# Copies of sums moved from GpSimd's queue to SyncE's, in a fused convolution and GELU feed-forward kernel

## The chip, the cores and the metric

The kernel runs on one core of a Trainium2 chip. The metric is the device time of one execution in microseconds (us), the median of several runs. A core has five engines that work side by side and meet only through semaphores: TensorE (PE: matrix products; its weight loads are listed as PEld), VectorE (DVE), ScalarE (ACT), GpSimd (POOL) and SyncE (SP). Transfers (DMAs) are issued by SP, ACT or POOL, in the order of that engine's program, and are carried out by 16 DMA engines that all queues share. A transfer tells of its landing by a semaphore.

## The reference

The input x has 8 sequences of 4096 tokens of 192 values. A causal convolution over 7 tokens comes first, whose weights are a softmax over the 7 taps, one set for each of 8 heads of 24 values. Then a feed-forward layer: 192 to 2048, exact GELU, 2048 to 192.

```
w = exp(w - max(w)); w = w / sum(w)                 # over the 7 taps of a head
x = sum over k of w[head, k] * x[token - 6 + k]     # zeros ahead of a sequence
h = x @ w_in                                        # 32768 x 192 @ 192 x 2048
g = 0.5 * h * (1 + erf(h / sqrt(2)))
out = g @ w_out                                     # 32768 x 2048 @ 2048 x 192
```

## The kernel before

The tokens are split into two halves of 16384, and both halves go through the core together: six blocks of 256 tokens of each half, then 29 blocks of 512, blocks 0 to 34. A block of 512 has 16 slots. In a slot TensorE makes 128 hidden columns for 512 tokens of both halves (`mm1`, line 991, into one of two buffers `hp`), and ScalarE applies GELU to them (line 896, into `gT`). Between the slots TensorE works on the second product of the block before, into four banks `ob`. So one block's second product runs beside the next block's first.

For each block VectorE transposes x (line 747), makes the taps of the convolution (line 775; ScalarE makes a first one, line 864), and brings the results of the second product to `osb` (lines 376 and 560), from where SyncE stores them.

Every second block from 8 to 32 (the list `ST`, 13 blocks) does its second product in a transformed way that needs fewer matrix products: instead of all products of parts of `gT` with parts of the weights, it multiplies sums of parts with sums of weights (`mm2_s`, line 1129). The rest take the plain way (`mm2_t`, line 1069). In what follows m is a transformed block; its sums are made while its own slots run, and TensorE uses them beside the slots of block m+1. A pair is block m and block m+1.

The sums are called S1, S3 (four parts each), Dn and S4 (two parts each) and lie in the buffers `sst`. S1 and S3 add two pieces of `gT`; Dn adds a piece of `gT` to S1; S4 adds one to Dn. Most parts are made by VectorE (`st_add`, line 487). Five of the parts of S1 and S3 are made by transfers instead (`BY_DMA`): a copy of one piece into `sst` (`st_dma` with h = 0, line 494) and then a transfer that adds the other piece onto it (h = 1, line 497). The copy waits for the GELU that makes its piece, the add for the copy's landing. TensorE waits for the add's landing before it uses that part (`wait_add`).

What each engine does in what order is fixed:

- GpSimd's list is sorted by a pair (block, slot). For each m it holds the five copies and five adds by `DMAS`: first number the place within block m, then sum, part, and copy (0) or add (1). Between them stand `halo` (lines 663 and 669), which carries six columns of x over to the next block, and `st_move`: a move of half a tile `p5s` at (m+1, 8.5) (line 504), and two later moves, `gsm` and `tq`, at (m+2, 2) and (m+2, 3).
- VectorE's order is written out by hand in `ORDER`, one letter an operation: c a convolution tap, t a transpose, 1, 3, d and 4 a part of S1, S3, Dn and S4, p a step of `st_post`, e a result brought out. `st_post` step 1 (line 538) waits for the landing of `p5s`; step 2 (line 541) must be done before TensorE begins the plain second product of block m+1.
- SyncE's list is also sorted by (block, place). In the steady part it holds for each pair: load of block m+4, store of m-2, load of m+5, store of m-1, each of four transfers of 192 KB. Before each of the four it waits until TensorE has finished the first slot of block m+1:

```
for at, op, n in sorted(work, key=lambda q: q[0]):
    if at[0] - 1 in ST:
        sp.wait_ge(S_MM1, SL0[at[0]] + 1)
    op(sp, n)
```

A load waits for its buffer (three of them, `xin`), a store for its results; VectorE waits for a store's landing before it writes the same `osb` (two of them) again.

Of the kernel before, what the change touches and what calls it, by code (L numbers as in the profile page):

```python
# [11 lines left out]
def bass_lightweight_conv__then__act_gelu_exact_kernel(  # L12
# [53 lines left out]
    SL0 = [sum(NSL[:n]) for n in range(NB + 1)]  # L66
# [5 lines left out]
    ST = list(range(M0 + 2, M1, 2))  # L72
# [43 lines left out]
    def sem(name):  # L116
        return es.enter_context(nc.semaphore(name))

    def ap(t, off, pat):
        return bass.AP(t, off, pat)  # L120

    with es:
# [53 lines left out]
        S_MM1 = sem("S_MM1")  # L176
# [10 lines left out]
        S_AC = sem("S_AC")  # L187
        S_DP = sem("S_DP")
        BY_DMA = [("S3", 0), ("S1", 0), ("S3", 1), ("S1", 1), ("S3", 2)]
        DMAS = [(3, "S3", 0, 0), (4, "S1", 0, 0), (7, "S3", 1, 0), (8, "S1", 1, 0), (8.1, "S1", 0, 1), (8.2, "S3", 0, 1),  # L190
                (9, "S1", 1, 1), (11, "S3", 2, 0), (11.1, "S3", 1, 1), (12, "S3", 2, 1)]
        S_CP = {k: sem("S_CP_%s_%d" % k) for k in BY_DMA}
        S_AD = {k: sem("S_AD_%s_%d" % k) for k in BY_DMA}
        S_PS = sem("S_PS")
# [66 lines left out]
        def part(q):  # L261

            return FQ * (0, 4, 2)[q], [[NP * F, 64], *([[F, NP]] if q < 2 else [[4 * FQ, 2 * NP]]), [1, FQ]]


        def cast(e, n, p):
            e.wait_ge(S_TR, NP * n + p + 1)
            dst = ap(xTb[PC[n]], p * XB + HX, [[NP * XB, 128], [1, WS[n]]])
            src = ap(xT[n % 2], p * XW + HX, [[NP * XW, 128], [1, WS[n]]])
            if n == 0:  # L270
                ins = e.activation(out=dst, in_=src, func=AF.Copy)
            else:
                ins = e.tensor_copy(dst, src)
            ins.then_inc(S_CAST[PC[n]])

        def dup(e, q, hf):

            c0, pat = part(q)
            e.wait_ge(S_WIN[(hf, 2 + 3 * hf, 3 + hf)[q]], 16)
            e.tensor_copy(  # L280
                ap(win, 64 * (1 - hf) * NP * F + c0 + FQ, pat), ap(win, 64 * hf * NP * F + c0, pat)
            ).then_inc(S_DUPP if (q, hf) == (0, 1) else S_DUPE)

        def trd(n):

            return NP * (n + 1) if n < 2 else 2 * NP + n - 1

        def cvd(n):

            return sum(NCV - 2 * (m in K0) for m in range(n + 1) if m not in PC)  # L290
# [100 lines left out]
        for (hf, cg), names in TILES.items():  # L391
            at = 0.0
# [6 lines left out]
        for e, (at, hf, cg, u, k) in enumerate(EVENTS):  # L399
            name = "DE" if u[0] in "DE" else u if u != "P3" else u + "LU"[cg]  # L400
# [161 lines left out]
        def load(e, n, qs=(0, 2, 1, 3), sm=None):  # L562
            mb = WS[n] // 32
            if n >= NX:
                e.wait_ge(S_TR, trd(n - NX))
            for q in qs:
                off = ((q // 2) * HALF + OFF[n]) * D + DQ * (q % 2)
                dst = [[TB // 32 * DQ, 32], [DQ, mb], [1, DQ]]
                src = [[D, 32], [32 * D, mb], [1, DQ]]
                e.dma_start(  # L570
                    ap(xin[n % NX], 32 * q * (TB // 32 * DQ), dst), ap(xt, off, src)
                ).then_inc(sm or S_XIN[n % NX], 16)

        def store(e, m):
# [28 lines left out]
        TAPS = ((5, 8, 11), (10, 12, 15))  # L603
        ORDER = (
            "tccccccccccccctccctccccccccccccwtcwcccccccccccwwwwctcccccccccccctcccccccccccccccccccccccccettceccccc"
            "cccccccccetccccecccccccetcecc1ccde1ed344ccccccpctpcpeccccccccpccececet1ccd3e1ed44ccccccpcccptpcecccc"
            "ccccpccececet1ccd3e1ed44ccccccpcccptpceccccccccpccececet1ccd3e1ed44ccccccpcccptpceccccccccpccececet1"
            "ccd3e1ed44ccccccpcccptpceccccccccpccececet1ccd3e1ed44ccccccpcccptpceccccccccpccececet1ccd3e1ed44cccc"
            "ccpcccptpceccccccccpccececet1ccd3e1ed44ccccccpcccptpceccccccccpccececet1ccd3e1ed44ccccccpcccptpceccc"
# [5 lines left out]
        @block.gpsimd  # L615
        def _(g):
            def win_in(q, hf, sm):
                c0, pat = part(q)
                g.dma_start(
                    ap(win, 64 * hf * NP * F + c0, pat), ap(wint, c0 + FQ * hf, pat)  # L620
                ).then_inc(sm, 16)

            g.wait_ge(S_MSET, 1)
            for hf in range(2):
                m = idb[64 * hf : 64 * hf + 64, :]
                g.affine_select(
                    out=m,
                    in_=m,
                    compare_op=ALU.is_equal,
                    fill=0.0,  # L630
                    base=0,
                    pattern=[[-1, 64]],
                    channel_multiplier=1,
                ).then_inc(S_IDN)
            g.wait_ge(S_IDN, 2)
            g.memset(wnm[:, :], 0.0).then_inc(S_WNM)
            g.memset(ap(xTb[0], HF, [[NP * XB, 128], [XB, NP], [1, HB]]), 0.0).then_inc(S_HALO)
            for q in range(2):
                for hf in range(2):
                    win_in(q, hf, S_WIN[(hf, 2 + 3 * hf)[q]])  # L640
            g.wait_ge(S_PRO, 9)
            g.tensor_tensor(
                ap(dg, 3 * 64, [[KS * 64, 128], [64, KS - 3], [1, 64]]),
                ap(idb, 0, [[64, 128], [0, KS - 3], [1, 64]]),
                ap(wcol, 3, [[32, 128], [1, KS - 3], [0, 64]]),
                ALU.mult,
            ).then_inc(S_DG)

            def wout_in(k):
                g0, gs = ((0, 1), (4, 1), (2, 4), (3, 4))[k]  # L650
                g.dma_start(
                    ap(wout, 2 * g0 * C, [[NF * C, 128], [2 * gs * C, 2], [1, 2 * C]]),
                    ap(woutt, 256 * g0 * C, [[2 * C, 128], [256 * gs * C, 2], [1, 2 * C]]),
                ).then_inc(S_WOUT[k], 16)

            def halo(n):

                t, tw = (xTb[PC[n]], XB) if n in PC else (xT[n % 2], XW)
                dst = ap(t, HF, [[NP * tw, 128], [tw, NP], [1, HB]])
                if n >= 4:  # L660
                    g.wait_ge(S_CV, cvd(n - 2))
                if OFF[n] % SEQ == 0:
                    g.memset(dst, 0.0).then_inc(S_HALO)
                    return
                g.wait_ge(S_TR, trd(n - 1))
                src = ap(
                    xT[(n - 1) % 2], HF + WS[n - 1], [[NP * XW, 128], [XW, NP], [1, HB]]
                )
                g.tensor_copy(dst, src).then_inc(S_HALO)  # L669

            win_in(2, 0, S_WIN[3])
            load(g, 2, (0,), S_XP)
            halo(1)
            g.wait_ge(S_HALO, 2)
            dup(g, 0, 1)
            win_in(2, 1, S_WIN[4])
            wout_in(0)
            load(g, 2, (2,), S_XP)
            g.wait_ge(S_DUPP, 1)
            cast(g, 1, 0)  # L680
            cast(g, 1, 1)
            load(g, 2, (1,), S_XP)
            wout_in(1)
            cast(g, 1, 2)
            load(g, 2, (3,), S_XP)
            wout_in(2)
            wout_in(3)
            halo(2)
            work = [((n - 2, 0), halo, n) for n in range(3, NB)]
            for m in ST:  # L690
                for at, name, q, h in DMAS:
                    work.append(((m, at), st_dma, g, m, name, q, h))
                work += [((m + 1, 8.5), st_move, g, m, 0), ((m + 2, 2), st_move, g, m, 1), ((m + 2, 3), st_move, g, m, 2)]
            for _, op, *rest in sorted(work, key=lambda q: q[0]):
                op(*rest)
# [498 lines left out]
        @block.sync  # L1194
        def _(sp):
            sp.dma_start(wsb[:, :], ap(wt, 0, [[KS, H], [1, KS]])).then_inc(S_WSB, 16)
            load(sp, 0, (0, 1))

            sp.wait_ge(S_PRO, 2)
            load(sp, 1)  # L1200
            sp.wait_ge(S_WOUT[3], 16)
            load(sp, 3)
            work = [((n - 3, 0), load, n) for n in range(4, ST[0] + 4)]
            work += [((p + 1, 1), store, p) for p in range(ST[0] - 2)]
            for m in [*ST, ST[-1] + 2]:
                work += [((m + 1, k), load, m + 4 + k) for k in range(2) if m + 4 + k < NB]
                work += [((m + 1, k + 0.5), store, m - 2 + k) for k in range(2) if m - 2 + k < M1]
            work += [((NB + 1, 0), store, p) for p in range(ST[-1] + 2, M1)]
            for at, op, n in sorted(work, key=lambda q: q[0]):
                if at[0] - 1 in ST:  # L1210
                    sp.wait_ge(S_MM1, SL0[at[0]] + 1)
                op(sp, n)
            for g in range(NG[NB - 1]):
                store_half(sp, g, 0)
            for s in range(2):
                sp.wait_ge(S_OUT[s], OUTS[NB - 1 if (NB - 1) % 2 == s else NB - 2])
# [28 lines left out]
```

## Time and profile before

| | |
|---|---|
| runs | 675.85, 672.76 and 675.66 us; median 675.66 |
| profiled execution | 671.07 us, of which the span of its instructions 669.3 |
| busy in the span | PE 663.9, DVE 612.1, ACT 594.3, POOL 189.6 us |
| copies, line 494 | 65, of 256 KB; issue 0.80 us each (mean) |
| adds, line 497 | 65, of 256 KB; issue 1.42 us each (mean) |
| copies and adds, issue to landing | 2.4 / 3.9 / 6.4 us (least, median, most) |
| loads of x and stores on SyncE, issue to landing | medians 4.8 and 4.6 us for 192 KB |

The profile is of one execution. Each engine's busy time, the idle time ahead of an instruction and what ended it are given; the chain is the run of work that ended last, followed back from the end. TensorE's clock was granted in full throughout (1.000). For a transfer the profile has the time in which the engine issued it and the moment at which it landed. A group of rows with `x3` is three instructions told together.

### The profile page before, as it was taken

To read this page: it belongs to the slowest core of one execution; us is meant where nothing else is said; L and a number is where in the kernel's file an instruction comes from. 1 tells how busy PE (TensorE), PEld (TensorE's weight loads), DVE (VectorE), ACT (ScalarE), POOL (GpSimd) and SP (SyncE) were. 2 spreads that over 40 slices of the span, in tenths; PEclk is the share of its full clock that TensorE was granted. 3 is DMA by queue.
4 is the path that set the end of the run, shared out by engine and by line. 5 is a ranking of instruction groups with operands and counts; after the bars stand their busy time and mean duration, and the time that the engine had idled before them with its cause. 6 is when DMAs were issued, how large, how long until landed. Compare 5 with 4: busy or idle time off the path is not lost.

```text
span 669.3 us, 27462 instructions
## 1 busy us (share of the span) xinstructions
PE 663.9 (99%) x12504; PEld 487.6 (73%) x12504; DVE 612.1 (91%) x704; ACT 594.3 (89%) x681; POOL 189.6 (28%) x230
## 2 busy tenths in 40 slices
PE   9999999999999999999999999999999999999998
PEld 8999655565655767678787777877767776777667
DVE  6999998889999999999999999999999999999621
ACT  8999988898998989989898998989979899898882
POOL 7000702315042250511505124150421504224000
PEclk9999999999999999999999999999999999999999
DMA  9435361967939479494886939569394693936333
GB/s 154 122 89 129 72 108 56 183 132 165 201 103 204 109 159 181 120 197 117 159 163 155 205 91 187 128 160 211 96 198 104 154 205 104 196 87 141 87 73 95
DMA packets 159075, 93.72 MB, mean 140 GB/s; under 512 B 129088, under 2 KB 152448, under 8 KB 158960
## 3 DMA queue, kind: packets, MB, share of 16 engines
q1 hardware_dynamic: 129136, 49.37, 35.5%
q0 software_dynamic: 28704, 42.02, 29.7%
q8 instruction: 98, 1.61, 1.0%
q10 hardware_dynamic: 1120, 0.59, 0.3%
q14 instruction: 17, 0.14, 0.1%
HBM read 28.31 MB, written 25.17 MB: 80 GB/s over the span
## 4 chain that ended last, share of the span: by engine, by line
PE 91%; DMA 4%; POOL 2%; issue 1%; ACT 1%; POOLq 0%
PE hp L991 46%; PE ob L1069 21%; PE ob L1129 17%; PE ob L1031 5%; DMA sst<-gT 4%; POOL sst L497 2%; PE ob L1185 1%; PE hp L1185 1%; PE hp L913 1%; POOL sst L494 1%; ACT gT L896 0%; PE ob L933 0%; PE ob L991 0%; ACT xc L243 0%; ACT osb L350 0%
## 5 line engine op out<-in xcount | busy, mean ns | idle before, releaser
L896 ACT ACTIVATE gT<-hp 128x1024 bf16<-128x1024 f32 x510 | 514.1, 1021 | 61.0 <-PE hp L991 54.7
L991 PE MATMUL hp<-xc,win 64*64 64x512 bf16 (+2 forms) x6036 | 440.1, 366 | 0.1
L775 DVE SCALAR_TENSOR_TENSOR acc<-xT,wcol,acc 128x1024 f32<-128x1024 f32 (+1 forms) x330 | 298.7, 972 | 4.6 <-ACT acc L864 3.9
L991 PEld LDWEIGHTS hp<-xc,win 64*64 64x64 bf16 (+1 forms) x6036 | 231.6, 106 | 90.9 <-ACT gT L896 7.8
L1069 PE MATMUL ob<-gT,wout 64*64 64x512 bf16 x2880 | 205.7, 376 | 0.0
L1129 PE MATMUL ob<-gT,wout 64*64 64x512 bf16 x1248 | 167.3, 376 | 0.0
L1069 PEld LDWEIGHTS ob<-gT,wout 64*64 64x64 bf16 x2880 | 113.2, 118 | 46.4
L1129 PE MATMUL ob<-sst,wst 64*64 64x512 bf16 x624 | 129.6, 376 | 2.1 <-DMA sst<-gT 2.1
L1129 PEld LDWEIGHTS ob<-gT,wout 64*64 64x64 bf16 x1248 | 83.6, 118 | 24.9
L497 POOL DMA_DIRECT2D sst<-gT x65 | 84.3, 1417 | 36.8 <-DMA sst<-gT 31.9
L747 DVE STREAM_TRANSPOSE xT<-xin 128x1536 f32<-128x1536 f32 (+2 forms) x39 | 74.7, 1925 | 1.6 <-DMA xin<-in_x_dram 1.4
L494 POOL DMA_DIRECT2D sst<-gT x65 | 52.2, 803 | 73.0 <-ACT gT L896 72.7
L775 DVE SCALAR_TENSOR_TENSOR xc<-xT,wcol,acc 128x1024 bf16<-128x1024 f32 (+1 forms) x66 | 61.6, 958 | 0.1
L487 DVE TENSOR_TENSOR sst<-gT,sst 128x2048 bf16<-128x2048 bf16 x52 | 61.4, 1231 | 0.1
L864 ACT ACTIVATE acc<-xT,wcol 128x512 f32<-128x512 f32 (+1 forms) x87 | 61.1, 702 | 0.0
L1129 PEld LDWEIGHTS ob<-sst,wst 64*64 64x64 bf16 x624 | 53.2, 107 | 7.7 <-DMA sst<-gT 3.5
L669 POOL COPY xT<-xT 128x18 f32<-128x18 f32 x30 | 28.0, 932 | 106.0 <-DVE xc L775 101.2
L1129 PE MATMUL ob<-gT,wst 64*64 64x512 bf16 x208 | 57.5, 376 | 0.0
L376 DVE STREAM_TRANSPOSE osb<-ob 128x512 f32<-128x512 f32 x45 | 40.6, 905 | 12.3 <-PE ob L1069 12.3
L1129 PE MATMUL ob<-sst,wout 64*64 64x256 bf16 x416 | 45.2, 269 | 0.0
L504 POOL DMA_DIRECT2D p5s<-p5s x13 | 7.4, 570 | 132.7 <-ACT p5s L525 132.7
L1031 PE MATMUL ob<-wout,gT 64*128 64x192 bf16 x768 | 41.9, 243 | 0.0
(74 smaller groups left out, 323.1 us busy)
## 6 DMA issues: line engine op xcount, KB each, us to landing
sst<-gT POOLq DMA_DIRECT2D x130, 256.0 KB, 3.9
out_dram<-osb SPq DMA_DIRECT2D x124, 192.0 KB, 4.6
xin<-in_x_dram SPq DMA_DIRECT2D x116, 192.0 KB, 4.8
tq<-uu POOLq DMA_DIRECT2D x13, 256.0 KB, 4.0
xin<-in_x_dram SPq DMA_DIRECT2D x18, 96.0 KB, 2.4
gsm<-uu POOLq DMA_DIRECT2D x13, 128.0 KB, 2.2
p5s<-p5s POOLq DMA_DIRECT2D x13, 64.0 KB, 4.8
wout<-in_moe_w_out_dram POOLq DMA_DIRECT2D x4, 192.0 KB, 4.5
```

The costliest lines, as they stand in the source:

```text
L376: v.transpose(osb_t(m, j), bank(BK[m][j])).then_inc(S_EV)
L487: v.tensor_tensor(out, one, two, ALU.add).then_inc(S_SA[NS.index(name)])
L494: e.dma_start(out, one).then_inc(S_CP[name, q], 16)
L497: e.dma_start(out, two, accum_op=ALU.add).then_inc(S_AD[name, q], 16)
L747: v.transpose(out, src).then_inc(S_TR)
L775: ins = v.scalar_tensor_tensor(dst, src, wk, a, op0=ALU.mult, op1=ALU.add)
L864: a.activation(out=acc[n % 2][:, p * TB : p * TB + w], in_=ap(xT[n % 2], p * XW + HX, [[NP * XW, 128], [1, w]]), func=AF.Copy, scale=wcol[ ...
L896: a.activation(out=ap(gT[n % 2], i * c * 2 * w, dst), in_=ap(ob, 2 * TB, [[4 * TB, 128], *src[1:]]) if u < SL0[1] and u % 3 == 2 else ap(h ...
L991: ins = t.matmul(hbuf(u, slice(fo, fo + fw), o, w), ap(win, f1, [[NP * F, 64], [2, fw]]), xc[n % 2][r, p * TB : p * TB + w], start=(p == 0 ...
L1031: ins = t.matmul(bb[sub], gT[m % 2][r, c0 : c0 + 128], wout[r, CH[sub][i] * C : (CH[sub][i] + 1) * C], start=(ph == 0 and k == 0), stop=(p ...
L1069: ins = t.matmul(bank(BK[m][j], slice(64 * h, 64 * h + 64), w), ap(wout, 64 * hf * NF * C + CH[h][i] * C + j, [[NF * C, 64], [NP, 64]],), ...
L1129: ins = t.matmul(bank(BK[m][bk], slice(64 * cg, 64 * cg + 64), w), wt_, a[r, c0 : c0 + w], start=(e == mine[0]), stop=(e in (mine[-1], GRO ...
```

## The change

The copies leave GpSimd's list and go to SyncE's, at the same places within block m. GpSimd keeps the adds only, in the order S3 part 0, S1 part 0, S1 part 1, S3 part 1, S3 part 2. SyncE's loads and stores of a pair wait for the fourth slot of block m+1 instead of the first; its copies do not wait for a slot, only for their GELU. In VectorE's order two letters change places, in the first transformed block alone: the first part of Dn comes ahead of one tap.

```diff
-        DMAS = [(3, "S3", 0, 0), (4, "S1", 0, 0), (7, "S3", 1, 0), (8, "S1", 1, 0), (8.1, "S1", 0, 1), (8.2, "S3", 0, 1),
-                (9, "S1", 1, 1), (11, "S3", 2, 0), (11.1, "S3", 1, 1), (12, "S3", 2, 1)]
+        COPIES = [(3, "S3", 0), (4, "S1", 0), (7, "S3", 1), (8, "S1", 1), (11, "S3", 2)]
+        ADDS = [(5, "S3", 0), (6, "S1", 0), (9, "S1", 1), (10, "S3", 1), (12.5, "S3", 2)]
...
-            "cccccccccetccccecccccccetcecc1ccde1ed344ccccccpctpcpeccccccccpccececet1ccd3e1ed44ccccccpcccptpcecccc"
+            "cccccccccetccccecccccccetcecc1cdce1ed344ccccccpctpcpeccccccccpccececet1ccd3e1ed44ccccccpcccptpcecccc"
...
-                for at, name, q, h in DMAS:
-                    work.append(((m, at), st_dma, g, m, name, q, h))
+                work += [((m, at), st_dma, g, m, name, q, 1) for at, name, q in ADDS]
...
+            work += [((m, at), st_dma, m, name, q, 0) for m in ST for at, name, q in COPIES]
...
-            for at, op, n in sorted(work, key=lambda q: q[0]):
+            for at, op, *rest in sorted(work, key=lambda q: q[0]):
                 if at[0] - 1 in ST:
-                    sp.wait_ge(S_MM1, SL0[at[0]] + 1)
-                op(sp, n)
+                    sp.wait_ge(S_MM1, SL0[at[0]] + 4)
+                op(sp, *rest)
```

## The prediction

> **What bounds the kernel now.** I read the page first, then the chain in order of time, the waits, and the timelines of POOL, SyncE, VectorE and TensorE over one pair of blocks. The page:
>
> ```profile
> PE 663.9 (99%) x12504; PEld 487.6 (73%) x12504; DVE 612.1 (91%) x704; ACT 594.3 (89%) x681; POOL 189.6 (28%) x230
> PE 91%; DMA 4%; POOL 2%; issue 1%; ACT 1%; POOLq 0%
> ```
>
> TensorE is hardly ever idle, so at most a few us can be won. The 4% of DMA and 2% of POOL in the chain look like 40 us, but most of that ran beside a busy TensorE: the chain only went through it where a wait ended last. The true loss is read from the rhythm of the chain:
>
> ```profile
> 110.18 0.86 PE ob L1069 x16
> ...
> 232.84 0.86 PE ob L1069 x16
> ...
> 273.43 0.86 PE ob L1069 x16
> ...
> 641.36 0.86 PE ob L1069 x16
> ```
>
> A pair of blocks takes 273.43 - 232.84 = 40.59 us undisturbed. Between 110.18 and 641.36 lie 13 pairs in 531.18 us; 13 x 40.59 is 527.67. So 3.5 us are lost to waits. The waits name them (us in total, times, longest):
>
> ```profile
> PEld ob L1129 <- DMA sst<-gT: 3.5, 3, 1.7
> DVE tq L538 <- DMA p5s<-p5s: 5.5, 8, 1.2
> ```
>
> Three waits of the weight loader on a transferred sum, 3.5 us, are all of it. The second line is on no path yet and returns below. How a sum comes to be late, in an undisturbed pair that begins at 431.14 (its transformed block m, then block m+1 from 451.67):
>
> ```profile
> 440.25 0.71 POOL L494 DMA_DIRECT2D sst<-gT  x1 [3.38 <-ACT gT L896]
> 441.55 0.71 POOL L494 DMA_DIRECT2D sst<-gT  x1 [0.59 <-ACT gT L896]
> 442.25 3.70 POOL L497 DMA_DIRECT2D sst<-gT  x3
> 445.66 1.04 POOL L494 DMA_DIRECT2D sst<-gT  x1
> 446.39 1.52 POOL L497 DMA_DIRECT2D sst<-gT  x1
> 450.47 1.18 POOL L497 DMA_DIRECT2D sst<-gT  x1 [2.56 <-DMA sst<-gT]
> ```
>
> L494 is a copy, L497 an add. The last copy (third part of S3) goes out at 445.66, behind three adds of the same queue; POOL then idles 2.56 us until it has landed, 450.2, and the last add goes out at 450.47. It lands 4.5 us later, 455.0 by the trace's landing times. TensorE asks for it at about 456.5: in the pair begun at 471.72 the loader waited 1.7 us until 498.80, so it had asked at 497.1, 25.4 us into the pair. So the margin is 1.5 us. In that pair the add started 1.7 us later than here (492.75) and took 6.00 us to land, and the margin was gone.
>
> **The change, part by part.**
>
> Copies on SyncE. A copy waits only for the gelu that makes its data; these end in this pair at 434.8, 436.0, 440.0, 441.3 and about 445.4. SyncE is free then: its last store of a pair goes out 34.7 us into the pair, so at 424.5 for the pair before (three slots later, 428.2), and has landed by 428.0 (431.7). POOL loses five issues of 0.72 us, 3.6 us a pair; POOL is 28% busy, so this alone is worth nothing. What counts is that the last copy is no longer in line behind adds. Its landing is shown nowhere for SyncE's ring. Bounds: 2.1 us (fastest load on that ring, half the size) and 6.6 us (slowest); the same copy on POOL's ring takes 2.4 at its fastest and 4.5 here. I take 3.3, nearest to the copy's own undisturbed row, with something for the two adds in flight. It lands at 445.4 + 3.3 = 448.7 instead of 450.2. At 6.6 it would land at 452.0.
>
> Adds as soon as their copy has landed. They are in the order S3, S1, S1, S3, S3; each costs POOL 1.25 us. With copies landed at 438, 439, 443, 444.3 and 448.7 POOL is never behind: the third and fourth are issued 444.3 to 446.8, the last at 448.8. It lands at 453.3 instead of 455.0: 1.7 us more margin, 3.2 in all. With the bound of 6.6 the add lands at 456.6, and the margin is gone. The waiting add holds up on POOL only the copying of six columns to the next block (L669, L663), which came after the last add before too. SyncE's waits hold up only copies and the next loads.
>
> A page of the Trainium skill speaks against this part: by "DMA: Bandwidth & Descriptors", section "Issuing engines are not separate DMA queues", transfers of all issuers run on the same 16 engines and a second issuer saves only issue time. By it the last sum comes 0.3 us earlier (445.66 against 445.4), and about 3 us of the lost 3.5 stay. I go by the 2.56 us of POOL's wait and by 4.5 against 2.4 us for the same copy, which say that the queue's order costs more than the issue.
>
> x and results three slots later. SyncE's 16 transfers of a pair (4 loads, 4 stores, twice) begin at 451.66, with the first slot of block m+1; the fourth slot ends 3.7 us later, 455.3. They fill the DMA engines:
>
> ```profile
> 431.14:451.67 20.53, 20.53 (x386) 15.54 (x382) 20.53 (x23) 18.39 (x21) 11.22 (x13) 1.00 0.59 137
> 451.67:471.72 20.05, 20.05 (x393) 15.40 (x388) 18.83 (x21) 18.80 (x22) 0.88 (x3) 1.00 0.94 176
> ```
>
> (columns: PE, PEld, DVE, ACT, POOL busy, clock, DMA share, GB/s.) The DMA share is 0.94 in block m+1 and 0.59 in block m. Later transfers leave the last add alone, worth nothing beyond the 3.5 us. What covers the delay: loads land 8.4 to 9.6 us before VectorE transposes them (5.8 in the first pair, 7.0 in the last), so at least 2.1 us are left; stores land 8.1 to 10.3 us before their buffer is written again, so 4.4 are left. Were that cover gone, each us late would be a us of VectorE's, which has about 1 us of idle time a pair.
>
> The one other thing in that traffic is the half-width move p5s (L504):
>
> ```profile
> 467.37 0.42 DVE L538 TENSOR_TENSOR tq<-ob,p5s 64x256 f32<-64x256 f32 x1 [1.09 <-DMA p5s<-p5s]
> ...
> 470.07 0.43 DVE L541 TENSOR_TENSOR tq<-ob,p5s 64x256 f32<-64x256 f32 x1
> ```
>
> ```profile
> 471.29 0.86 PE L1069 MATMUL ob<-gT,wout 64*64 64x512 bf16 x12
> ```
>
> ```profile
> DMA to landing us min/median/max: 1.9/4.8/5.2
> ```
>
> The first two rows are VectorE's timeline, the third TensorE's, the last the landing times of the tile p5s. VectorE sits idle until p5s lands (36.2 us into the pair); after it come a transpose and L541, which ends at 470.50 and must be done before TensorE's L1069 matmuls at 471.29. That is 0.8 us of slack. The move's issue stays at 31.1 us into the pair, where SyncE's own transfers now take 4.4 us to land; shifted by 3.7 us it meets the state of 27.4 us, where they take 5.0 to 5.1. So p5s lands 0.6 us later, still inside 0.8; without the last add in the engines it may be less. Bounds: 0.3 us earlier and 1.9 later (the slowest store, 6.1, plus the 0.5 by which p5s lags SyncE's). For pairs that scatter above 0.8 I put 0.5 us in all.
>
> A rule would strike this term out: by "DMA: Bandwidth & Descriptors", section "Queues, rings and completion order", each DMA engine takes turns between queues packet by packet, so a small move need not stand behind a long ring. The trace disagrees: 1.9 us where the ring was empty, 4.8 in traffic. By the rule the sum would be 0.5 us lower.
>
> The swapped step in VectorE's order (first transformed block only) puts one sum of 1.2 us ahead of one tap of 0.9 us. VectorE has idled 1.7 and 1.4 us in that block: nothing, or 0.3 us either way.
>
> Sum: 671.07 (span 669.3 and 1.8 around it) - 3.5 + 0.5 = 668.1 us for the profiled execution.
>
> **Against the median.** The runs shown are 672.76 to 675.85, median 675.66, 4.6 above the profiled one. No view says where these 4.6 us lie. If around the program, the new median is 675.66 - 3.0 = 672.7; if they are more of the same waits (0.35 us a pair), it is 668.1. Spread of 3 us between runs of one program speaks for waits in part; I take the middle, 670.5.
>
> **The rivals.** A change of 0.5% (3.4 us) is about what a measurement of this kernel can tell from none.
>
> First, the gain is real but too small: the waits go only partly, or the 4.6 us are fixed. For it: three waits in 13 pairs are all there is to see. 673 to 677.
>
> Second, slower: p5s. If it lands d later, each of 12 pairs stalls TensorE by d - 0.8 (the last pair's traffic is shorter, 8 transfers). At d = 1.9 that is 13 us, 683 us; it decides from d = 1.2, where 12 x 0.4 eats the gain. For it: 0.8 us is thin and VectorE has no other idle time, so the delay also reaches its own sums. Against: the growth from 4.4 to 5.1.
>
> Third, SyncE's ring is slow for copies (6.6 us), so that the last sum lands 1.6 us later than before. With 1.6 added to the 13 landings of this trace (22.9 to 27.0 us into their pairs, against 25.4) the waits come to 10 us instead of 3.5: 682 us. Against: the ring is empty when copies go out.
>
> **How the numbers follow.** Forecast 0.58 (667 to 673, of which 0.04 within 0.5%), first rival 0.24, second 0.12, third 0.06. Under 672.3 is faster: 0.54; up to 679 the same: 0.28 and 0.01 of each slower case, 0.30; the rest slower, 0.16. For 8 in 10: 666 (all waits gone, p5s as by its early bound) to 677 (first rival whole, little of the others).
>
> **What would show it.** Right: no TensorE wait on a transferred sum; the last add about 17.7 us into a pair instead of 19.3; SyncE's loads from 24.2; p5s still landing by 36.8 and L541 ending before L1069 asks; pairs of 40.6 us throughout. Wrong: a pair longer than 40.6 with TensorE released by VectorE's L541 (second rival) or by a sum's DMA (third), or equal pairs and an unchanged median (first).

## The result

The changed kernel takes 683.13 us (median of 4 runs, 681.37 to 684.25) against 675.41 us before in the same comparison: the ratio is 1.012, with a 95% interval of 1.0084 to 1.0156. The forecast was 670.5 us, range 666 to 677, with 16% for slower. It was wrong, in size and in sign. The profiled execution of the changed kernel has a span of 679.6 us, 10.3 more than the one of before.

In the changed kernel's line numbers, line 991 of before is 990, 1069 is 1068 and 1129 is 1128. Two lines of its page, and four rows of its chain in order of time:

```profile
PE 669.1 (98%) x12504; PEld 500.7 (74%) x12504; DVE 613.5 (90%) x704; ACT 594.5 (87%) x681; POOL 143.3 (21%) x165
PE 65%; DMA 7%; DVE 5%; ACT 1%; issue 1%; DVEq 0%
```

```profile
194.27 0.86 PE ob L1068 x16
...
235.66 0.86 PE ob L1068 x16
276.25 0.86 PE ob L1068 x16
...
610.54 0.86 PE ob L1068 x16
```

The ten pairs between 194.27 and 610.54 take 41.63 us each, 1.04 more than the undisturbed 40.59. One of them, from 235.66 to 276.25, takes 40.59: the floor has not moved. Taken over all 13 pairs by the starts of the blocks' first GELUs, 13.3 us are lost where 3.4 were lost before; the rest of the 10.3 is 0.4 us ahead of the first transformed block. VectorE has entered the chain (5%), and the waits say where (us in total, times, longest):

```profile
POOL sst L497 <- DMA sst<-gT: 140.1, 28, 15.3
DVE sst L487 <- DMA sst<-gT: 15.1, 12, 1.8
PEld ob L1128 <- DVE tq L534: 9.3, 12, 1.3
PEld ob L1128 <- DVE sst L487: 8.1, 11, 1.3
...
DVE tq L538 <- DMA p5s<-p5s: 2.4, 4, 1.0
...
PEld ob L1128 <- DMA sst<-gT: 0.2, 1, 0.2
```

The wait that the change was to remove is gone: TensorE's loader waits 0.2 us for transferred sums instead of 3.5. In its place VectorE waits 15.1 us for a transferred sum, which was no wait worth listing before, and TensorE then waits for VectorE at two places: for a part of a sum made by VectorE (line 487; the fourth part of S1) and for the step of line 534 ten us later. VectorE's own slack, its wait for `p5s`, has shrunk from 5.5 us to 2.4.

What VectorE waits for is the add of S1 part 1: the first part of Dn needs both transferred parts of S1. The timelines of GpSimd, SyncE and VectorE in the pair that begins at 397.90:

```profile
405.80 2.44 POOL L497 DMA_DIRECT2D sst<-gT  x2 [4.45 <-DMA sst<-gT]
414.34 3.65 POOL L497 DMA_DIRECT2D sst<-gT  x3 [6.10 <-DMA sst<-gT]
```

```profile
401.56 11.18 SPq L494 DMA_DIRECT2D sst<-gT  x5
```

```profile
415.01 0.76 DVE L487 TENSOR_TENSOR sst<-gT 128x1024 bf16<-128x1024 bf16 x1
415.57 2.05 DVE L774 SCALAR_TENSOR_TENSOR acc<-xT,wcol,acc 128x512 f32<-128x512 f32 x2
418.14 1.23 DVE L487 TENSOR_TENSOR sst<-gT,sst 128x2048 bf16<-128x2048 bf16 x1 [0.51 <-DMA sst<-gT]
```

SyncE issues the five copies at their GELUs, without a wait of its own. The two adds of 405.80 (7.9 us into the pair; before, adds began at 11.1) start early, as intended. But the copy of S1 part 1, issued at 408.04, lands only at 414.06, and GpSimd stands idle for 6.10 us before the next three adds go out together. The add of S1 part 1 lands at 418.02, and VectorE has waited for it. The DMA engines are left partly idle just then: their share is 0.58 in the changed kernel and 0.98 in the one before. The same stretch of a pair, 16 to 20 us from its start, in the changed kernel and in the one before (PE, PEld, DVE, ACT, POOL busy, clock, DMA share, GB/s):

```profile
413.90:417.90 4.00, 4.00 (x80) 3.07 (x76) 3.73 (x4) 3.40 (x4) 3.56 (x4) 1.00 0.58 105
```

```profile
406.40:410.40 4.00, 4.00 (x80) 3.04 (x76) 4.00 (x5) 3.40 (x4) 1.66 (x3) 1.00 0.98 193
```

Medians over the 13 pairs, in us from the start of the pair, by the landing times in the traces:

| | before | changed | forecast |
|---|---|---|---|
| adds begin | 11.1 | 7.9 | 6.9 |
| copy of S1 part 1: issue, landing | 10.4, 13.4 | 10.1, 15.8 | 10.1, 13.2 |
| add of S1 part 1 lands | 17.8 | 19.9 | not worked out |
| first part of Dn begins on VectorE | 19.2 | 20.1 | not worked out |
| copy of S3 part 2 lands | 19.0 | 16.8 | 17.6 |
| add of S3 part 2: issue, landing | 19.3, 23.9 | 17.6, 23.1 | 17.7, 22.2 |

The undisturbed pair (from 230.71) is the one in which the add of S1 part 1 landed earliest, at 18.8; its copy had landed at 14.8.

Theory A, formed from this: the two early adds lie in the DMA engines ahead of the later copies; the copy of S1 part 1 lands late, so does its add, VectorE waits for it and TensorE pays. Against it stand theory B, that copies are slow on SyncE's ring in themselves, and theory C, that the later loads and stores do the harm.

### The profile page after: what moved, and what is told of

It is laid out like the page before. It is cut to its first block, busy times and chain, and to the rows that moved or that the text cites. A ratio compares the mean times of both kernels' runs of the same rounds, so it can differ in the third digit from the quotient of the medians.

```text
span 679.6 us, 27462 instructions
## 1 busy us (share of the span) xinstructions
PE 669.1 (98%) x12504; PEld 500.7 (74%) x12504; DVE 613.5 (90%) x704; ACT 594.5 (87%) x681; POOL 143.3 (21%) x165
## 4 chain that ended last, share of the span: by engine, by line
PE 65%; DMA 7%; DVE 5%; ACT 1%; issue 1%; DVEq 0%
PE hp L990 32%; PE ob L1128 16%; PE ob L1068 16%; DMA sst<-gT 7%; DVE sst L487 2%; DVE tq L534 1%; ACT gT L895 1%; PE ob L1184 1%; PE hp L1184 1%; DVE osb L376 1%; DVE acc L774 0%; DVE xc L774 0%; ACT osb L350 0%; DVEq L458 0%
## 5 line engine op out<-in xcount | busy, mean ns | idle before, releaser
L990 PE MATMUL hp<-xc,win 64*64 64x512 bf16 (+2 forms) x6036 | 463.6, 366 | 0.4 <-DVE xc L774 0.3
L990 PEld LDWEIGHTS hp<-xc,win 64*64 64x64 bf16 (+1 forms) x6036 | 246.6, 106 | 84.8 <-ACT gT L895 7.6
L1068 PE MATMUL ob<-gT,wout 64*64 64x512 bf16 x2880 | 209.1, 376 | 0.0
L1128 PE MATMUL ob<-gT,wout 64*64 64x512 bf16 x1248 | 183.6, 378 | 0.0
L1068 PEld LDWEIGHTS ob<-gT,wout 64*64 64x64 bf16 x2880 | 122.5, 118 | 37.5
L1128 PE MATMUL ob<-sst,wst 64*64 64x512 bf16 x624 | 131.8, 377 | 3.1 <-DVE sst L487 3.1
L497 POOL DMA_DIRECT2D sst<-gT x65 | 79.2, 1520 | 140.2 <-DMA sst<-gT 140.1
L1128 PEld LDWEIGHTS ob<-gT,wout 64*64 64x64 bf16 x1248 | 89.8, 118 | 16.1
L487 DVE TENSOR_TENSOR sst<-gT,sst 128x2048 bf16<-128x2048 bf16 x52 | 60.8, 1208 | 15.1 <-DMA sst<-gT 15.1
L1128 PEld LDWEIGHTS ob<-sst,wst 64*64 64x64 bf16 x624 | 52.2, 107 | 15.3 <-DVE sst L487 8.1
L669 POOL COPY xT<-xT 128x18 f32<-128x18 f32 x30 | 33.3, 1109 | 114.3 <-DVE xc L774 109.0
L1128 PE MATMUL ob<-sst,wout 64*64 64x256 bf16 x416 | 46.6, 269 | 0.0
L1128 PEld LDWEIGHTS ob<-sst,wout 64*64 64x64 bf16 x416 | 37.7, 119 | 1.0
```

What stands on the lines that cost most here:

```text
L487: v.tensor_tensor(out, one, two, ALU.add).then_inc(S_SA[NS.index(name)])
L497: e.dma_start(out, two, accum_op=ALU.add).then_inc(S_AD[name, q], 16)
L990: ins = t.matmul(hbuf(u, slice(fo, fo + fw), o, w), ap(win, f1, [[NP * F, 64], [2, fw]]), xc[n % 2][r, p * TB : p * TB + w], start=(p == 0 ...
L1068: ins = t.matmul(bank(BK[m][j], slice(64 * h, 64 * h + 64), w), ap(wout, 64 * hf * NF * C + CH[h][i] * C + j, [[NF * C, 64], [NP, 64]],), ...
L1128: ins = t.matmul(bank(BK[m][bk], slice(64 * cg, 64 * cg + 64), w), wt_, a[r, c0 : c0 + w], start=(e == mine[0]), stop=(e in (mine[-1], GRO ...
```

## The experiments

Ratios are to the kernel before on the same chip, with 95% intervals. "Lost" is the sum over the 13 pairs above the undisturbed lengths of their second blocks (20.05 us each), in the profiled execution: 3.4 us before, 13.3 in the changed kernel.

**Adds held back.**

```diff
-        ADDS = [(5, "S3", 0), (6, "S1", 0), (9, "S1", 1), (10, "S3", 1), (12.5, "S3", 2)]
+        ADDS = [(5, "S1", 1), (6, "S1", 0), (9, "S3", 0), (10, "S3", 1), (12.5, "S3", 2)]
```

> The changed kernel, with its adds in the order S1 part 1, S1 part 0, S3 part 0, S3 part 1, S3 part 2, so that no add goes out before the copy of S1 part 1 has landed. Theory A (the adds that now start at 8 to 9 us into a pair fill the DMA engines, the copy of S1 part 1 lands at 16 instead of 13.3 us, its add at 20 instead of 17.8, VectorE waits for it 1.3 us a pair and TensorE then waits for VectorE twice): that copy lands by 13.5, its add by 17.5, VectorE waits for no add, span 666 to 671 us instead of 679.6. Theory B (a copy on SyncE's ring is slow in itself): the copy still lands at about 16, all five adds are later still, span 685 us or more. Theory C (the later loads and stores do the harm): span 677 to 682, as in the changed kernel.

690.77 us, ratio 1.0249 (1.0197 to 1.0300); lost 21.6 us. A miss: the time is what theory B forecast, and the copy and its add land a little later than theory A said. And yet the copy answers: with no add ahead it lands at 13.8, 3.6 us after its issue instead of 5.7, and not at 16 as by theory B. Theory B is refuted on this point. What I had overlooked is the rest of the queue:

```profile
417.71 6.12 POOL L497 DMA_DIRECT2D sst<-gT  x5 [10.41 <-DMA sst<-gT]
```

All five adds now go out in one run, and land at 18.3, 20.8, 22.2, 23.6 and 24.9 us: after the first two, one every 1.3 to 1.5 us. The first part of Dn also needs the add of S1 part 0, now the second, and begins at 20.9; TensorE waits 7.5 us for transferred sums as well.

**Loads and stores from the first slot again.**

```diff
-                    sp.wait_ge(S_MM1, SL0[at[0]] + 4)
+                    sp.wait_ge(S_MM1, SL0[at[0]] + 1)
```

> The changed kernel, with loads and stores issued from the first slot of block m+1 again, as before the change. Theory A: the add of S1 part 1 still lands at about 20 us into a pair, VectorE still waits 1 to 1.5 us for it; time 681 to 690 us, since the last adds now meet the loads. Theory C: back to the time before, 672 to 677 us. Theory B says the same as A here.

682.80 us, ratio 1.0124 (1.0075 to 1.0174); VectorE waits 15.3 us for sums, the add of S1 part 1 lands at 20.2. As A said; theory C is refuted.

**The later loads and stores alone**, on the kernel before:

```diff
-                    sp.wait_ge(S_MM1, SL0[at[0]] + 1)
+                    sp.wait_ge(S_MM1, SL0[at[0]] + 4)
```

> The kernel before, with one change alone: loads and stores three slots later. Theory A: the sums land as before or earlier (the last add meets no loads), TensorE's waits for transferred sums (3.5 us) go, VectorE's p5s waits stay about 1 us; span 665.5 to 668 us instead of 669.3. Theory C: slower than before, span 674 to 680, with TensorE or VectorE waiting for p5s or x. Theory B: as A.

670.28 us, ratio 0.9938 (0.9916 to 0.9960); lost 1.6 us. TensorE's loader waits 0.2 us for transferred sums. The span of the profiled execution, 669.6, missed the range for a reason of its own: its first transformed block began at 107.0 us instead of 105.1. This part of the change makes the kernel faster.

**VectorE's order altered**, so that it comes to the first part of Dn later. In eleven of the thirteen transformed blocks as shown here, and in the first of them the swap is undone:

```diff
-1ccd3e1ed44
+1cc3de1ed44
```

> The changed kernel, with VectorE's order altered: the last part of S3, which needs no transfer, comes before the first part of Dn, which needs the add of S1 part 1 (and the swap in the first transformed block is undone). Transfers are as in the changed kernel. Theory A: the add still lands at about 20 us, but VectorE comes to it only at about 20.2 and waits at most 0.3 us; TensorE's waits for VectorE (8 us for the fourth part of S1 and 9 us for the step of line 534) go mostly; span 667 to 672. If the wait on that add were not what delays TensorE, the span stays at 677 to 682.

677.37 us, ratio 1.0030 (0.9997 to 1.0062); lost 9.7 us. Half a hit. VectorE waits 5.9 us for sums instead of 15.1, and 3.2 us more for the GELU that the last part of S3 needs; TensorE's wait on its sums falls from 8.1 to 4.2 us, but that on line 534 stays at 8.2. VectorE is still 0.9 us later than before when it has done its sums (27.3 against 26.5 us into the pair), and line 534 has no slack for that. The span of the profiled execution, 678.0, lies outside the range for theory A and inside the one for its rival; as VectorE's wait went only in part, this run alone does not decide between them.

**One add ahead instead of two.**

```diff
-        ADDS = [(5, "S3", 0), (6, "S1", 0), (9, "S1", 1), (10, "S3", 1), (12.5, "S3", 2)]
+        ADDS = [(5, "S1", 0), (6, "S1", 1), (9, "S3", 0), (10, "S3", 1), (12.5, "S3", 2)]
```

> The changed kernel, with its adds in the order S1 part 0, S1 part 1, S3 part 0, S3 part 1, S3 part 2: one add instead of two lies in the DMA engines ahead of the copy of S1 part 1. Theory A, as the held adds left it (copy of S1 part 1 at 13.8 with no add ahead, 15.8 with two, 13.4 before; the first part of Dn needs both adds of S1): that copy lands at 14.3 to 15.0, its add at 18.3 to 19.0, the add of S1 part 0 long before, VectorE waits 0 to 0.3 us a pair instead of 1.2, time 670 to 675 us, better than the changed kernel's 683. Against A, if the add of S1 part 1 is late because every add on this queue now takes longer whatever lies ahead: it lands at 20 again and the time stays at 680 to 685.

678.62 us, ratio 1.0063 (1.0034 to 1.0092); lost 9.4 us. The direction of the copy is A's, the rest was missed: the copy lands at 15.1, just beyond the range given, but its add at 19.8, hardly earlier than in the changed kernel, and VectorE still waits 10.5 us for sums. The reason given against A is not it: this add takes 4.3 us from issue to landing, against 4.2 in the changed kernel and 4.1 before (medians). It is late because it is issued late, at 15.5. From issue to landing this copy takes 3.6 us with no add ahead, 5.0 with one and 5.7 with two: the first does two thirds of the harm.

**VectorE held, transfers untouched**, on the kernel before:

```diff
-            v.wait_ge(S_GELU, done)
+            v.wait_ge(S_GELU, SL0[m] + NF if (name, q) == ("Dn", 0) else done)
```

> The kernel before, all transfers as they were, with VectorE's first part of Dn held in every transformed block until that block's last GELU, 20.5 us into the pair, where it had begun at 19.2 and in the changed kernel at 20.1. No transfer is touched. Second half of theory A (a wait of VectorE at this place, whatever its cause, is paid by TensorE at the fourth part of S1 and at the step of line 534): VectorE waits 1.2 to 1.4 us a pair, the 13 pairs lose 12 to 17 us instead of 3.4, time 683 to 690 us. If TensorE lost its time to something else in the change: 673 to 678 us.

687.02 us, ratio 1.0190 (1.0149 to 1.0231); lost 18.9 us. Its waits:

```profile
DVE sst L487 <- ACT gT L896: 22.1, 13, 1.9
...
PEld ob L1129 <- DVE sst L487: 10.9, 13, 0.9
PEld ob L1129 <- DVE tq L534: 8.6, 10, 1.3
```

No transfer was touched, and the same two waits of TensorE appear as in the changed kernel, with VectorE's idle time of 22.1 us ahead of them (1.7 a pair, more than the 1.2 to 1.4 expected, hence the larger loss). The second half of A is shown: idle time of VectorE at this place is paid by TensorE for the most part; 15 us more are lost for 22 us of it.

**Adds at their old times, copies on SyncE, loads late.**

```diff
-        ADDS = [(5, "S3", 0), (6, "S1", 0), (9, "S1", 1), (10, "S3", 1), (12.5, "S3", 2)]
+        ADDS = [(8.1, "S1", 0), (8.2, "S3", 0), (9, "S1", 1), (11.1, "S3", 1), (12, "S3", 2)]
...
+                work += [((m, 8), g.wait_ge, S_GELU, SL0[m] + 8)]
```

> The changed kernel, with its adds in the order of before and none issued until the GELU that the copy of S1 part 1 waits for (10.1 us into the pair), so that they go out at about the times of before; copies stay on SyncE and loads stay late. Theory A: the copy of S1 part 1 lands at 13.5 to 14.3, its add at 18.0 to 18.7, VectorE waits under 0.3 us a pair, the last add lands by 23.5, time 669 to 674 us. If copies on SyncE's ring do harm without early adds too: 678 us or more.

671.98 us, ratio 0.9961 (0.9938 to 0.9984); lost 4.3 us. Copy and add of S1 part 1 land at 13.8 and 18.6 us, the last add at 22.3, VectorE waits 1.7 us for sums in all. Of the parts of the change the early start of the adds, in its new order, does the harm; start and order were not tried apart here. Without it the change is a gain.

**The last copy alone moved**, on the kernel before:

```diff
-                (9, "S1", 1, 1), (11, "S3", 2, 0), (11.1, "S3", 1, 1), (12, "S3", 2, 1)]
+                (9, "S1", 1, 1), (11.1, "S3", 1, 1), (12, "S3", 2, 1)]
...
+            work += [((m, 11), st_dma, m, "S3", 2, 0) for m in ST]
```

> The kernel before, with the last copy alone (S3 part 2) moved to SyncE's ring; all adds and the other copies in their order on GpSimd's, loads and stores from the first slot as before. This is the part of the change that the forecast counted on. It expected the copy to land 1.5 us earlier and the last add 1.7 us earlier: copy at 16.7 to 17.5 instead of 19.0, last add at 21.5 to 22.7 instead of 23.9, no TensorE wait on a transferred sum (3.5 us before), VectorE as before; time 668 to 672.5 us. If moving the copy doesn't help: 673 to 677.

670.25 us, ratio 0.9950 (0.9926 to 0.9975); lost 3.1 us, nearly all of it in two pairs, in one of which the loader still waited 2.0 us for a transferred sum. The copy lands at 17.5 instead of 19.0 and the add at 22.9 instead of 23.9 (medians): the forecast's 1.5 us for the copy was right, its 1.7 us for the add was 1.0. That this version is faster rests on the medians of its runs: its profiled execution loses hardly less than the one before (3.4).

**That copy and the later loads together**: the edit just shown, and

```diff
-                    sp.wait_ge(S_MM1, SL0[at[0]] + 1)
+                    sp.wait_ge(S_MM1, SL0[at[0]] + 4)
```

> The kernel before, with the two parts that each made it faster alone: the last copy (S3 part 2) on SyncE's ring, and loads and stores three slots later. Each removes most of TensorE's waits on the last sum, so they should not add up: theory A says the waits on sums go entirely, ratio to the time before 0.990 to 0.994, median 667.5 to 671, and a smaller spread between runs than the 8.5 us of before. If the two gains were of different kinds they would add: ratio 0.987 to 0.990.

671.60 us, ratio 0.9973 (0.9950 to 0.9995). A miss: the two gains do not add, and the sum is no better than either. No wait on a transferred sum is left on TensorE, but it waits 4.0 us for line 534, against 0.7 with the copy alone; `p5s` lands at 36.1 us into the pair instead of 35.5 (medians).

**The move of the copies alone**: the changed kernel with the adds at their old times, as in the experiment on them, and the loads and stores from the first slot.

```diff
-        ADDS = [(5, "S3", 0), (6, "S1", 0), (9, "S1", 1), (10, "S3", 1), (12.5, "S3", 2)]
+        ADDS = [(8.1, "S1", 0), (8.2, "S3", 0), (9, "S1", 1), (11.1, "S3", 1), (12, "S3", 2)]
...
+                work += [((m, 8), g.wait_ge, S_GELU, SL0[m] + 8)]
...
-                    sp.wait_ge(S_MM1, SL0[at[0]] + 4)
+                    sp.wait_ge(S_MM1, SL0[at[0]] + 1)
```

> The changed kernel, with adds held as before (order of before, none ahead of the GELU of the copy of S1 part 1) and loads and stores from the first slot as before: the move of the copies alone. Theory A: copy and add of S1 part 1 as with adds held and loads late (13.8 and 18.6 us into the pair), last add by 23.5, VectorE waits under 0.3 us a pair, time 669 to 674 us, ratio 0.993 to 0.999. If the copies do harm unless loads are late: 677 us or more.

669.81 us, ratio 0.9957 (0.9938 to 0.9976), 8 runs from 668.15 to 671.13; span of the profiled execution 667.1, lost 1.0 us. As A said. Its timeline of GpSimd, in the pair that begins at 390.52, and its waits:

```profile
400.94 2.44 POOL L497 DMA_DIRECT2D sst<-gT  x2 [6.95 <-ACT gT L896]
403.93 2.42 POOL L497 DMA_DIRECT2D sst<-gT  x2 [0.55 <-DMA sst<-gT]
408.99 1.20 POOL L497 DMA_DIRECT2D sst<-gT  x1 [2.64 <-DMA sst<-gT]
```

```profile
PEld ob L1129 <- DVE tq L534: 1.4, 3, 0.9
DVE sst L487 <- DMA sst<-gT: 1.0, 2, 0.8
```

The first two adds go out 10.4 us into the pair, 2.5 us later than in the changed kernel, and the next two 13.4 us into it, 3.0 us earlier than there (16.4). Starting two transfers later lets the two that matter start sooner.

All five versions that leave the adds at their old times beat both kernels, with ratios of 0.9938 to 0.9973 and intervals that overlap, so no order among them is claimed. Their profiled executions lose 1.0 to 4.3 us in the pairs, and that of the kernel before, which was a quick one, 3.4; so the profiles do not show where the gain in the medians comes from.

## Why the prediction was wrong, point by point

**The step that failed** is "with copies landed at 438, 439, 443, 444.3 and 448.7 POOL is never behind: the third and fourth are issued 444.3 to 446.8". I gave the last copy 3.3 us "with something for the two adds in flight", but the third and fourth copies about 3 us, as if nothing were ahead of them, though by my own schedule the first two adds had gone out just before. Measured, the fourth copy took 5.7 us; without adds ahead it took 3.6 (the first experiment). In the pair shown GpSimd stood still for 6.10 us, and the third add went out 16.4 us into the pair instead of 13.2.

**The second fault** goes with it: I asked of each sum only when TensorE wants it. The list of who waits for the adds was not made, and the sum 671.07 - 3.5 + 0.5 has no term for a wait of VectorE on one; measured, VectorE waits 15.1 us and 13.3 us are lost instead of 3.4. VectorE's Dn waits for both adds of S1, at 19.2 us, with 1.4 us of margin (17.8); after it come a part of S1 and line 534, which TensorE waits for with little or no slack. I had written that VectorE has about 1 us of idle time a pair, and in the second rival that it has no other, and did not apply it here. The held VectorE shows the price: 15 us more lost for 22 us of its idle time.

**What was right.** The waits of TensorE on transferred sums went, 3.5 to 0.2 us. The last copy off GpSimd's queue lands earlier; moved alone it is a gain. That the last add goes out at 17.6 us (forecast 17.7) is luck: its copy has landed at 16.8, and the add goes out third in the run of three that the late fourth copy set off. It lands at 23.1 us, where the forecast had 22.2. The 2.4 us that the prediction called this copy's fastest on GpSimd's queue is the fastest of any copy there; its own fastest was 3.7. Transfers three slots later are covered: in the transformed pairs of the changed kernel loads land at least 4.4 us before their transpose, stores at least 5.7 us before their buffer is written again, and in the changed kernel itself they neither help nor harm (ratio 1.012 with them, 1.0124 without). VectorE's swap in the first transformed block, for which the prediction had nothing, or 0.3 us either way, was not tried alone; it may cost more. In the version with the copies alone moved, which keeps it, 0.9 of the 1.0 us lost lie in that block, where VectorE waits 0.80 us for the transferred sum that the swap makes it need sooner.

**The rivals.** The second, `p5s`, was not the cause: it lands 0.2 us later in the changed kernel (36.2 against 36.0 us into the pair, medians), and its list of waits has none of TensorE on line 541, so the 0.5 us of the sum were not paid. The 0.6 us that I gave it does show where the adds keep their old times, 36.2 with late loads against 35.7 without, copies on SyncE in both; these two profiled executions differ by 3.3 us in what is lost, against 0.5 in the forecast, but their ratios do not differ. The third rival named the right kind of loss, a sum that lands later, with the wrong sum and the wrong cause: with the adds at their old times and the loads early, the first four copies on SyncE's ring land at most 0.4 us later than they did on GpSimd's queue (medians), and the last one earlier.

**The two rules weighed.** The page "DMA: Bandwidth & Descriptors" of the Trainium skill, section "Issuing engines are not separate DMA queues", says that a second issuer saves only issue time. The moved last copy, 1.5 us earlier where issue accounts for 0.3, shows more than that. But its ground, the same DMA engines for all queues, is what sank the change: adds from GpSimd's queue delayed copies on SyncE's. The rule of turns between queues, packet by packet (the same page, section "Queues, rings and completion order"), holds here in part, and passing is not cheap. In the pair from 397.90 of the changed kernel these are the packets, MB and share of the DMA engines' time of GpSimd's queue (q0, adds) and SyncE's ring (q1, copies), first from 407.4 to 409.0, then from 410.0 to 411.5:

```profile
q0 software_dynamic: 247, 0.25, 98.5%
...
q1 hardware_dynamic: 5, 0.01, 1.2%
```

```profile
q0 software_dynamic: 182, 0.19, 77.4%
q1 hardware_dynamic: 167, 0.17, 40.0%
```

While the first add runs, the third copy, issued at 406.75, gets no turns to speak of. The second add and the fourth copy then take turns nearly one for one, but by these rows a packet of the add holds an engine for 102 ns and one of the copy for 57, so that the copy has little more than a third of the engines' time. They share the engines like this in ten of the 13 pairs.

**Against the median.** I took half of the 4.6 us between the profiled execution and the median as waits. The runs have a span each, and time less span is 1.7 to 1.9 us in all: the 4.6 us lie within the span. The profiled execution of before was one of the quickest: on one chip 22 runs with the clock at 1.000 go from 670.49 to 677.50. Part of this is the start: the first transformed block began at 105.05 us in it, and at 105.2 to 107.4 in the eleven other kernels' profiles.

**What stays open.** Why the copy pays 1.4 us for a single add ahead and only 0.7 for a second one is not settled, nor why a copy now stands behind a whole add and now takes turns with it; the traces do not tell one DMA engine's packets from another's. Nor is it shown how much of the spread of the kernel before comes from sums that land at the edge, though all versions that are faster spread less: the standard deviation of their runs is 1.0 to 1.7 us, that of the kernel before 2.0 to 2.4 on the same chips.

## What to carry to other kernels

A transfer that starts earlier than its reader needs it takes the DMA engines from one that is urgent: order transfers by when their readers want them, and before calling an early start free look for the transfers that will be in flight beside it. List every engine that waits for a moved result, not only the one that the profile shows waiting, and ask of each how much slack it has; an engine 91% busy in the page had about 1 us in 40. Test the parts of a change one by one: here the moved copies and the later loads were each a small gain, and the early adds turned the whole into a loss.

## What the runs showed of the hardware that was not expected

A copy of 256 KB takes 2.4 us from issue to landing at its quickest, on SyncE's ring as on GpSimd's queue. When five adding transfers of 256 KB went out in a row (the adds held back), they landed one every 1.3 to 1.5 us after the first two. A copy on SyncE's ring took 3.6, 5.0 and 5.7 us with none, one and two adds of GpSimd's queue ahead. And 21 runs of the kernel before on one chip differ by 8.8 us with TensorE's clock at 1.000 throughout, while the eight runs of the version with the copies alone moved, on the same chip, lie within 3.0 us.
